# Softmax probabilities scaled tile by tile on GpSimd, a first pair loaded in groups, and later row sums

## The chip, the cores and the metric

The kernel runs on one core of one Trainium2 chip. The metric is the device time of one execution in microseconds (us); the median of three runs stands for the kernel. All times here are us unless marked ns. The engines are PE (TensorE's matmuls; PEld are its weight loads), DVE (VectorE), ACT (ScalarE), POOL (GpSimd) and SP (SyncE, which only issues DMAs here).

## What is computed

Three layers follow one another on 4 batches of 576 tokens. The first is an attention of 8 heads of 64: four heads with a local mask of 32 positions, four with a strided mask.

```python
scores = scale * np.matmul(q, k.transpose(0, 1, 3, 2))
scores = np.where(masks[None, :, :, :], scores, -1000000000.0)
scores = scores - np.max(scores, axis=-1, keepdims=True)
attn = np.exp(scores)
attn = attn / (np.sum(attn, axis=-1, keepdims=True) + 1e-09)
return np.matmul(attn, v).astype(np.float32)
...
theta = x @ w_theta
zr, zi = x * np.cos(theta), x * np.sin(theta)
y = np.einsum('ts,bsd->btd', w_tok_r, zr) + np.einsum('ts,bsd->btd', w_tok_i, zi)
u = x + y
x = u + np.maximum(u @ w_ch, 0.0)
```

The second layer, in the lower lines, mixes tokens with two 576x576 matrices and channels with one of 512x512. The third is a mixture of 4 causal attention experts, of which each token takes two.

## The kernel before

**Attention.** Only blocks that the masks leave are computed. Two heads go together as a pair (pairs 0 and 1 local, 2 and 3 strided), and a pair is cut into three groups of tiles: local tiles are 128 rows (64 queries of two heads) by 96 keys, three in a group; strided tiles are 108 rows by 54 keys, four, four and three in a group. `load_pair` loads q, k and the three v pieces of a pair with one DMA each. `attn_pair` does for every group: PE adds the mask (L185) and the scores `s` (L189) in PSUM; DVE takes the maximum `mx` (L203 or L210); ACT takes the exponential into `p`. Where `per_tile` holds (batch 0 but for pair 2, and the first group of each pair of batch 1), ACT does it tile by tile and adds up the rows itself (L206); else DVE subtracts (L211), ACT does all tiles in one instruction (L213), and DVE sums the rows (L214). DVE adds 1e-9 and takes the reciprocal `sm` (L215, L216). L217 multiplies all tiles of `p` at once by `sm`, spread over the columns: DVE does it in batch 0, GpSimd in batches 1 to 3. PE transposes the tiles of `p` into `tp` (L220), ACT or DVE copies them to `pt` (L224), PE multiplies with v into `av` (L243), and `av` is copied into X (L248, L250).

**Mixing.** Per batch and half h: `theta` (matmuls L265 to L267 on `th`, three for each product, since every factor is split into a high and a low part), sines on ACT, `rotate` (`xn` transposes L311, products `cs` on DVE, high and low parts `zhi`, `zlo`), and `tokens` (the matmuls on `y`, whose sums DVE adds to X at L350). `channels` follows one batch later, with the matmuls on `g`: eight groups of 12 matmuls, named g_b_m_n, in two PSUM buffers; DVE drains each with L372. The weights arrive as 64-bit numbers in pieces (`load64`) and are converted by ACT (L139, L102) and DVE (L140, L104, L106) during batch 0.

**Experts.** From about 350 us on; their code is not touched.

**Order.** Each engine runs its instructions in a fixed order. It is made when the program is built, by a scheduler that plays a timeline of all engines; `tc.issue_after` holds an instruction back until another is issued. So each edit can move instructions on every engine. The attention of batch b+1 is woven between the mixing of batch b. SP issues DMAs in its own fixed order, and one that waits for a buffer holds up those behind it.

Of the kernel before, what the change touches and what calls it, by code (L numbers as in the profile page):

```python
# [19 lines left out]
ALU = mybir.AluOpType  # L20
AX = mybir.AxisListType
PSUM = bass.MemoryType.PSUM

B, S, DM, HD, NE = 4, 576, 512, 64, 4
NT = 5
TW = [128, 128, 128, 128, 64]
HALF = S // 2
# [20 lines left out]
def fused_kernel(ctx: ExitStack, tc: tile.TileContext, ql, kl, vl, qs, ks, vs, wth, wtk, wch, wqk, wvg, wo, out):  # L48
    nc = tc.nc
# [95 lines left out]
    def per_tile(b, pair, g):  # L145

        return b == 0 and pair != 2 or b == 1 and g == 0
# [3 lines left out]
    def load_pair(b, pair, ain, qbufs, kbufs):  # L151
        local = pair < 2
        pj = pair % 2
        groups, rw, kw = (LOCAL, LQ, LK) if local else (STRIDED, RQ, RQ)
        nq = groups[-1][1]

        qt = ain.tile([128, 11 * 2 * RQ], F32, tag="q", bufs=qbufs, name=f"q_{b}_{pair}")
        qt = qt[:, :nq * 2 * rw].rearrange("p (n q) -> p n q", n=nq)
        kt = ain.tile([128, S + WPAD], F32, tag="k", bufs=kbufs, name=f"k_{b}_{pair}")
        kn = S + WPAD if local else S  # L160
        nc.sync.dma_start(qt, (ql if local else qs)[b, pj])
        nc.sync.dma_start(kt[:, :kn], (kl if local else ks)[b, pj])
        vgs = []
        for g, (j0, j1) in enumerate(groups):
            vg = ain.tile([128, 4, 2, HD], F32, tag="v", name=f"v_{b}_{pair}_{g}")
            nc.sync.dma_start(vg[:kw, :j1 - j0], (vl if local else vs)[b, pj, :, j0:j1])
            vgs.append(vg)
        loaded[b, pair] = qt, kt, vgs

    def attn_pair(b, pair, ps1, apl, deep):  # L170
        ps_of[b] = ps1
        local = pair < 2
        groups, rw, kw = (LOCAL, LQ, LK) if local else (STRIDED, RQ, RQ)
        qt, kt, loads = loaded[b, pair]
        xo = X[b][:, pair, :]
        done = []
        for g, (j0, j1) in enumerate(groups):
            vg = loads[g]
            n = j1 - j0

            wd = [min(rw, S - rw * j) for j in range(j0, j1)]
            mask = mask_l[:, min(g, 1):min(g, 1) + 3, :] if local else mask_s[:, 2 * (g // 2):2 * (g // 2) + n, :]
            rm = 2 * rw
            s = ps1.tile([128, 512], F32, tag="s", bufs=2 * deep, name=f"s_{b}_{pair}_{g}")
            nc.tensor.matmul(s[:rm, :n * kw], twice[pair // 2], mask, start=True, stop=False)  # L185
            for i in range(n):
                k0 = rw * (j0 + i)
                w = kw if local else wd[i]
                nc.tensor.matmul(s[:rm, i * kw:i * kw + w], qt[:, j0 + i, :], kt[:, k0:k0 + w], start=False, stop=i == n - 1)  # L189
            mx = apl.tile([128, 4], F32, tag="mx", name=f"mx_{b}_{pair}_{g}")  # L190
            sm = apl.tile([128, 4], F32, tag="sm", name=f"sm_{b}_{pair}_{g}")

            ss = s[:, 384:388] if per_tile(b, pair, g) else sm
            p = apl.tile([128, 3 * LK], F32, tag="p", name=f"p_{b}_{pair}_{g}")

            def tiles(v):
                return v[:rm, :n * kw].rearrange("p (n k) -> p n k", n=n)

            def each(v):
                return v[:rm, :n, None].to_broadcast([rm, n, kw])  # L200

            if per_tile(b, pair, g):
                peaks[b] = nc.vector.tensor_reduce(mx[:rm, :n], tiles(s), axis=AX.X, op=ALU.max, negate=True).ins  # L203
                nc.scalar.activation(mx[:rm, :n], mx[:rm, :n], AF.Copy, scale=SCALE)
                for i in range(n):
                    powers[b] = nc.scalar.activation(p[:rm, i * kw:(i + 1) * kw], s[:rm, i * kw:(i + 1) * kw], AF.Exp,  # L206
                                                     bias=mx[:rm, i:i + 1], scale=SCALE,
                                                     accum_out=ss[:rm, i:i + 1]).ins
            else:
                nc.vector.tensor_reduce(mx[:rm, :n], tiles(s), axis=AX.X, op=ALU.max)  # L210
                nc.vector.tensor_tensor(tiles(p), tiles(s), each(mx), op=ALU.subtract)  # L211
                with tc.issue_after(sins[b - 1, pair // 2]) if (b > 1 and pair % 2) else nullcontext():
                    nc.scalar.activation(p[:rm, :n * kw], p[:rm, :n * kw], AF.Exp, scale=SCALE)  # L213
                nc.vector.tensor_reduce(sm[:rm, :n], tiles(p), axis=AX.X, op=ALU.add)  # L214
            nc.vector.tensor_scalar_add(sm[:rm, :n], ss[:rm, :n], 1e-9)  # L215
            nc.vector.reciprocal(sm[:rm, :n], sm[:rm, :n])  # L216
            (nc.vector if b == 0 else nc.gpsimd).tensor_tensor(tiles(p), tiles(p), each(sm), op=ALU.mult)  # L217
            tp = ps1.tile([128, 512], F32, tag="t", bufs=deep, name=f"tp_{b}_{pair}_{g}")
            for i in range(n):
                turned = nc.tensor.transpose(tp[:kw, i * rm:(i + 1) * rm], p[:rm, i * kw:(i + 1) * kw],  # L220
                                             ident[:rm, :rm])
            pt = apl.tile([128, 8 * RQ], F32, tag="pt", name=f"pt_{b}_{pair}_{g}")
            copy = nc.vector.tensor_copy if b == 0 and g == 1 else nc.scalar.copy
            copy(pt[:kw, :n * rm], tp[:kw, :n * rm])  # L224
            done.append((j0, pt[:, :n * rm].rearrange("p (n h q) -> p n h q", n=n, h=2), wd, vg))
            if b == 0 or g == 2:

                for part in (done,) if b == 0 else (done[:2], done[2:]):
                    values(b, pair, part, xo, turned)
                done = []  # L230
# [33 lines left out]
    def mm3(ps, ahi, alo, bhi, blo, first, last):  # L264
        nc.tensor.matmul(ps, ahi, bhi, start=first, stop=False)  # L265
        nc.tensor.matmul(ps, ahi, blo, start=False, stop=False)  # L266
        return nc.tensor.matmul(ps, alo, bhi, start=False, stop=last)  # L267
# [66 lines left out]
            eng = nc.gpsimd if b > 0 else nc.vector  # L334
            halved[b, h] = eng.tensor_tensor(lo, zf, f(hi), op=ALU.subtract).ins  # L335

    us = {}

    def tokens(b, h):
        for n in range(2):  # L340
# [21 lines left out]
    def channels(b):  # L362
        for n in range(2):
            sl = slice(HALF * n, HALF * (n + 1))
            for m in range(4):
                g = ps1.tile([128, 512], F32, tag="acc", bufs=2, name=f"g_{b}_{m}_{n}")
                ms = slice(128 * m, 128 * m + 128)
                for c in range(4):
                    mm3(g[:, :HALF], wch_hi[:, c, ms], wch_lo[:, c, ms], us[c][0][:, sl], us[c][1][:, sl],
                        c == 0, c == 3)  # L370
                u = X[b][:, m, sl]
                nc.vector.scalar_tensor_tensor(u, g[:, :HALF], 0.0, u, op0=ALU.max, op1=ALU.add)  # L372

    halfpi = const.tile([128, 1], F32, name="halfpi")
    nc.gpsimd.memset(halfpi, math.pi / 2)
# [416 lines left out]
```

## Time and profile before

| | us |
|---|---|
| median of 3 runs (lowest, highest) | 556.71 (555.69, 557.0) |
| profiled execution | 555.94 |
| its span, first to last instruction | 553.8 |
| busy in the span: PE | 529.7 |
| busy: DVE, ACT, GpSimd | 400.9, 315.9, 188.5 |

The span is what the profile's views show; the profiled execution's time is 2.1 us longer. A line such as L217 is a line of the kernel before. Windows give each engine's busy time in a stretch and the clock that TensorE was granted in it (1.00 is 2.4 GHz, 0.50 is 1.2 GHz). The chain of waits follows the work that ended last back from the end. In a timeline, a bracket holds the engine's idle time before the instruction and what ended it.

### The profile page before, as it was taken

Reading aid. Unit: us, or ns where it says so; the run is one execution under the profiler, and the core shown is the slowest. Engines: PE = TensorE matmul, PEld = TensorE weight load, DVE = VectorE, ACT = ScalarE, POOL = GpSimd, SP = SyncE. Lnnn points to the kernel's source line nnn. Section 1 sums busy time; section 2 is a strip of 40 time slices with the busy share of each in tenths; the row PEclk is TensorE's granted clock in tenths of the full one; section 3 lists DMA queues with packets and bytes.
Section 4 is the critical chain, followed back from the end, with each engine's and each line's share of the span. In section 5 each row is a group of like instructions: output and inputs, shape, how many; then the busy total and the mean of one; then the engine's idle time right before and its main releaser. Section 6 shows DMA issues by size and latency. Waiting matters only on the chain.

```text
span 553.8 us, 12475 instructions
## 1 busy us (share of the span) xinstructions
PE 529.7 (96%) x4536; PEld 507.0 (92%) x4536; DVE 400.9 (72%) x1222; ACT 315.9 (57%) x904; POOL 188.5 (34%) x273
## 2 busy tenths in 40 slices
PE   6898999998999999999999999989999999999987
PEld 5778899998999999999999998879989999999987
DVE  4979997675775567675456443798988898888972
ACT  4977984426363163452246321576687767767873
POOL 1000013321562113551015533254456434625451
PEclk9959999999999999999999999999999999999999
DMA  9957243560202131001000011000001001100012
GB/s 286 320 180 262 81 161 107 168 197 1 90 23 68 32 132 33 24 24 43 17 0 1 28 33 40 1 1 2 1 10 59 22 1 44 44 2 11 33 45 86
DMA packets 20389, 37.53 MB, mean 68 GB/s; under 512 B 2904, under 2 KB 12296, under 8 KB 20328
## 3 DMA queue, kind: packets, MB, share of 16 engines
q1 hardware_dynamic: 20328, 36.73, 20.4%
q8 instruction: 36, 0.59, 0.5%
q14 instruction: 25, 0.20, 0.1%
HBM read 32.01 MB, written 4.72 MB: 66 GB/s over the span
## 4 chain that ended last, share of the span: by engine, by line
PE 74%; DVE 12%; ACT 8%; DMA 2%; issue 2%; POOL 1%; SPq 0%; DVEq 0%; POOLq 0%; ACTq 0%
PE y L265 7%; PE y L266 7%; PE y L267 7%; PE s L189 6%; PE av L243 4%; PE tp L220 3%; PE tp L624 3%; PE g L265 3%; PE g L267 3%; PE g L266 3%; PE th L265 3%; PE th L267 3%; PE th L266 2%; DVE nm L603 2%; PE o L580 2%; PE s L598 2%
## 5 line engine op out<-in xcount | busy, mean ns | idle before, releaser
L265 PE MATMUL y<-wtk_hi,zhi 128*128 128x288 f32 x288 | 85.8, 300 | 1.5 <-DVE cs L289 1.1
L266 PE MATMUL y<-wtk_lo,zhi 128*128 128x288 f32 x288 | 85.8, 298 | 0.0
L267 PE MATMUL y<-wtk_hi,zlo 128*128 128x288 f32 x288 | 85.3, 297 | 0.0
L217 POOL TENSOR_TENSOR p<-p,sm 128x288 f32<-128x288 f32 (+2 forms) x36 | 22.4, 628 | 150.3 <-PE y L267 73.2
L621 POOL TENSOR_SCALAR p<-p,sm,gt 128x256 f32<-128x256 f32 (+1 forms) x64 | 45.2, 709 | 52.5 <-DVE sm L619 32.5
L614 ACT ACTIVATE p<-s,nm 128x128 f32<-128x128 f32 (+2 forms) x96 | 49.6, 518 | 14.2 <-DVE nm L603 7.8
L265 PEld LDWEIGHTS y<-wtk_hi,zhi 128*128 128x128 f32 x288 | 54.0, 188 | 1.9 <-ACT wtk_hi L102 1.2
L266 PEld LDWEIGHTS y<-wtk_lo,zhi 128*128 128x128 f32 x288 | 54.2, 188 | 0.1
L335 POOL TENSOR_TENSOR zlo<-cs,zhi 128x512 fp32r<-128x512 f32 (+1 forms) x30 | 35.8, 1208 | 54.0 <-DVE zhi L331 43.2
L267 PEld LDWEIGHTS y<-wtk_hi,zlo 128*128 128x128 f32 x288 | 54.1, 188 | 0.1
L265 PE MATMUL th<-wth_hi,x_hi 128*128 128x256 f32 (+1 forms) x160 | 47.9, 300 | 0.6 <-ACT X L250 0.5
L603 DVE TENSOR_REDUCE nm<-s 128x1 f32<-128x128 f32 (+2 forms) x96 | 44.2, 468 | 5.5 <-PE s L601 4.4
L266 PE MATMUL th<-wth_lo,x_hi 128*128 128x256 f32 (+1 forms) x160 | 46.0, 288 | 0.0
L267 PE MATMUL th<-wth_hi,x_lo 128*128 128x256 f32 (+1 forms) x160 | 45.8, 290 | 0.0
L189 PE MATMUL s<-k,q 128*108 128x54 f32 (+2 forms) x320 | 42.8, 274 | 1.5 <-DMA k<-in_kl 1.5
L189 PEld LDWEIGHTS s<-k,q 128*108 128x108 f32 (+1 forms) x320 | 40.7, 196 | 2.5 <-issue 2.4
L224 ACT COPY pt<-tp 96x384 f32<-96x384 f32 (+2 forms) x44 | 21.0, 478 | 37.9 <-PE tp L220 37.6
L265 PE MATMUL pq<-x_hi,wqk_hi 128*128 128x288 f32 x128 | 39.8, 311 | 1.1 <-DVE q L549 1.0
L261 POOL TENSOR_TENSOR x_lo<-X,x_hi 128x576 fp32r<-128x576 f32 x20 | 29.8, 1495 | 32.2 <-DVE x_hi L259 25.8
L265 PE MATMUL g<-u_hi,wch_hi 128*128 128x288 f32 x128 | 38.9, 304 | 1.4 <-DVE X L372 1.4
L633 DVE TENSOR_TENSOR ptlo<-tp,pthi 128x128 fp32r<-128x128 f32 (+4 forms) x80 | 37.6, 478 | 1.2 <-ACT pthi L632 0.6
L266 PE MATMUL pq<-x_lo,wqk_hi 128*128 128x288 f32 x128 | 38.0, 297 | 0.0
(173 smaller groups left out, 1702.6 us busy)
## 6 DMA issues: line engine op xcount, KB each, us to landing
X<-in_wtk SPq DMA_DIRECT2D x18, 287.8 KB
q<-in_qs SPq DMA_DIRECT2D x8, 594.0 KB
q<-in_ql SPq DMA_DIRECT2D x8, 576.0 KB
v<-in_vl SPq DMA_DIRECT2D x24, 144.0 KB
out_t<-X SPq DMA_DIRECT2D x20, 128.0 KB
k<-in_kl SPq DMA_DIRECT2D x8, 304.0 KB
k<-in_ks SPq DMA_DIRECT2D x8, 288.0 KB
X<-in_wth SPq DMA_DIRECT2D x8, 255.8 KB
```

The lines of the kernel that those rows point to most:

```text
L189: nc.tensor.matmul(s[:rm, i * kw:i * kw + w], qt[:, j0 + i, :], kt[:, k0:k0 + w], start=False, stop=i == n - 1)
L217: (nc.vector if b == 0 else nc.gpsimd).tensor_tensor(tiles(p), tiles(p), each(sm), op=ALU.mult)
L243: nc.tensor.matmul(av[64 * h:64 * h + 64, c0:c0 + wi], vg[:w, i, h, :], pt[:w, i, h, :wi], start=True, stop=True)
L261: halved[name] = eng.tensor_tensor(lo, x, f(hi), op=ALU.subtract).ins
L265: nc.tensor.matmul(ps, ahi, bhi, start=first, stop=False)
L266: nc.tensor.matmul(ps, ahi, blo, start=False, stop=False)
L267: return nc.tensor.matmul(ps, alo, bhi, start=False, stop=last)
L335: halved[b, h] = eng.tensor_tensor(lo, zf, f(hi), op=ALU.subtract).ins
L603: nc.vector.tensor_reduce(nm[:w, t + ci:t + ci + 1], s[:w, :c1 - c0], axis=AX.X, op=ALU.max, negate=True)
L614: nc.scalar.activation(p[:w, c0:c1], scs[ci][:w, :c1 - c0], AF.Exp, bias=nm[:w, t:t + 1], scale=1.0, accum_out=acc)
L621: eng.tensor_scalar(p[:w, :kn], p[:w, :kn], sm[:w, t:t + 1], gt[:w, t, e:e + 1], op0=ALU.mult, op1=ALU.mult)
L633: nc.vector.tensor_tensor(dst(ptlo), src, f(dst(pthi)), op=ALU.subtract)
```

## The change

Three things change. The first pair of batch 0 is loaded by groups: q and k come in three DMAs each, a group of q and then the part of k that it needs. For pair 1 of batches 2 and 3, the row sums (L217 now) are held back until DVE's drain of the matmul group g of block 0 and second half (`gated[b - 2, 1, 0]`, now L377) is issued. The multiplication by the reciprocal is done by GpSimd in all batches, one instruction for each tile, with a column of `sm` as a scalar for each row (now L222) in place of one instruction for a group.

```diff
-        nc.sync.dma_start(qt, (ql if local else qs)[b, pj])
-        nc.sync.dma_start(kt[:, :kn], (kl if local else ks)[b, pj])
+        for j0, j1 in groups if (b, pair) == (0, 0) else [(0, nq)]:
+            nc.sync.dma_start(qt[:, j0:j1], (ql if local else qs)[b, pj, :, j0:j1])
+            k0, k1 = j0 * rw + (kn - S if j0 else 0), kn if j1 == nq else j1 * rw + kn - S
+            nc.sync.dma_start(kt[:, k0:k1], (kl if local else ks)[b, pj, :, k0:k1])
...
-                nc.vector.tensor_reduce(sm[:rm, :n], tiles(p), axis=AX.X, op=ALU.add)
+                with tc.issue_after(gated[b - 2, 1, 0]) if (b > 1 and pair == 1) else nullcontext():
+                    nc.vector.tensor_reduce(sm[:rm, :n], tiles(p), axis=AX.X, op=ALU.add)
             nc.vector.tensor_scalar_add(sm[:rm, :n], ss[:rm, :n], 1e-9)
             nc.vector.reciprocal(sm[:rm, :n], sm[:rm, :n])
-            (nc.vector if b == 0 else nc.gpsimd).tensor_tensor(tiles(p), tiles(p), each(sm), op=ALU.mult)
+            for i in range(n):
+                cols = p[:rm, i * kw:(i + 1) * kw]
+                nc.gpsimd.tensor_scalar(cols, cols, sm[:rm, i:i + 1], 1.0, op0=ALU.mult, op1=ALU.mult)
...
-                nc.vector.scalar_tensor_tensor(u, g[:, :HALF], 0.0, u, op0=ALU.max, op1=ALU.add)
+                gated[b, n, m] = nc.vector.scalar_tensor_tensor(u, g[:, :HALF], 0.0, u, op0=ALU.max, op1=ALU.add).ins
```

The order of the instructions moves on every engine in the first 350 us. On PE the experts' part keeps its order, but for one of the last output blocks. Three places follow; names end with a buffer's number, which differs between the programs, and the numbers ahead of it are batch, pair and group (p, sm, s, tp, pt), or batch, m and n (g).

DVE in batch 0, pair 2, around the third group's subtraction; first before, then now.

```order
L140 SCALAR_TENSOR_TENSOR X2_63<-X1_62,X2_63 128x256
L211 TENSOR_TENSOR p_0_2_2_438<-s_0_2_2_431,mx_0_2_2_436 108x162
L214 TENSOR_REDUCE sm_0_2_1_405<-p_0_2_1_406 108x4
L140 SCALAR_TENSOR_TENSOR X2_63<-X3_64,X2_63 128x256
L224 COPY pt_0_1_1_305<-tp_0_1_1_301 96x384
L217 TENSOR_TENSOR p_0_2_0_373<-p_0_2_0_373,sm_0_2_0_372 108x216
```

```order
L266 TENSOR_TENSOR x0_0_0_lo_634<-X0_61,x0_0_0_hi_633 128x576
L219 RECIPROCAL sm_0_2_0_388<-sm_0_2_0_388 108x4
L229 COPY pt_0_1_1_319<-tp_0_1_1_315 96x384
L213 TENSOR_TENSOR p_0_2_2_460<-s_0_2_2_453,mx_0_2_2_458 108x162
L218 TENSOR_SCALAR sm_0_2_1_424<-sm_0_2_1_424 108x4
L140 SCALAR_TENSOR_TENSOR X2_63<-X1_62,X2_63 128x256
```

The subtraction into p_0_2_2 stood three rows ahead of the copy of tp_0_1_1 and now stands behind it; the multiplication of p_0_2_0 is gone from DVE.

DVE in batch 1, up to the first reciprocal, sm_1_0_0, whose scaled tiles PE transposes first; first before, then now.

```order
L215 TENSOR_SCALAR sm_1_0_0_995<-s_1_0_0_989 128x3
L214 TENSOR_REDUCE sm_1_0_1_1017<-p_1_0_1_1018 128x3
L140 SCALAR_TENSOR_TENSOR X2_63<-X3_64,X2_63 128x256
L104 TENSOR_TENSOR wtk_lo_113<-X2_63,wtk_hi_112 128x288
L104 TENSOR_TENSOR wch_lo_115<-X2_63,wch_hi_114 128x256
L360 TENSOR_TENSOR u_0_0_lo_1288<-X0_61,u_0_0_hi_1287 128x288
L360 TENSOR_TENSOR u_0_1_lo_1292<-X0_61,u_0_1_hi_1291 128x288
L211 TENSOR_TENSOR p_1_0_2_1039<-s_1_0_2_1032,mx_1_0_2_1037 128x288
L216 RECIPROCAL sm_1_0_0_995<-sm_1_0_0_995 128x3
```

```order
L218 TENSOR_SCALAR sm_1_0_0_1027<-s_1_0_0_1021 128x3
L104 TENSOR_TENSOR wtk_lo_113<-X2_63,wtk_hi_112 128x288 x2
L340 TENSOR_TENSOR zlo_0_1_4_961<-cs_0_1_4_919,zhi_0_1_4_960 128x256
L140 SCALAR_TENSOR_TENSOR X2_63<-X3_64,X2_63 128x288
L217 TENSOR_REDUCE sm_1_0_1_1051<-p_1_0_1_1052 128x3
L212 TENSOR_REDUCE mx_1_0_2_1073<-s_1_0_2_1068 128x3
L140 SCALAR_TENSOR_TENSOR X2_63<-X3_64,X2_63 128x256
L219 RECIPROCAL sm_1_0_0_1027<-sm_1_0_0_1027 128x3
```

The reciprocal was row 180 of DVE's program and is now row 159: twelve of the 21 rows less are the multiplications of batch 0, and nine are conversions, subtractions and low parts that now come later.

DVE in batch 2, around the row sums of pair 1; first before, then now.

```order
L372 SCALAR_TENSOR_TENSOR X0_61<-g_0_2_0_1911,X0_61 128x288
L321 TENSOR_TENSOR cs_1_0_1_1723<-cs_1_0_1_1723,xn_1_0_1_2003 128x512
L214 TENSOR_REDUCE sm_2_1_0_2052<-p_2_1_0_2053 128x3
L214 TENSOR_REDUCE sm_2_1_1_2073<-p_2_1_1_2074 128x3
L215 TENSOR_SCALAR sm_2_1_0_2052<-sm_2_1_0_2052 128x3
L214 TENSOR_REDUCE sm_2_1_2_2094<-p_2_1_2_2095 128x3
L372 SCALAR_TENSOR_TENSOR X0_61<-g_0_3_0_1925,X0_61 128x288
L215 TENSOR_SCALAR sm_2_1_1_2073<-sm_2_1_1_2073 128x3
L216 RECIPROCAL sm_2_1_0_2052<-sm_2_1_0_2052 128x3
```

```order
L377 SCALAR_TENSOR_TENSOR X0_61<-g_0_2_0_1977,X0_61 128x288
L326 TENSOR_TENSOR cs_1_0_1_1783<-cs_1_0_1_1783,xn_1_0_1_2069 128x512
L377 SCALAR_TENSOR_TENSOR X0_61<-g_0_3_0_1991,X0_61 128x288
L377 SCALAR_TENSOR_TENSOR X0_61<-g_0_0_1_2005,X0_61 128x288
L217 TENSOR_REDUCE sm_2_1_0_2118<-p_2_1_0_2119 128x3
L217 TENSOR_REDUCE sm_2_1_1_2141<-p_2_1_1_2142 128x3
L217 TENSOR_REDUCE sm_2_1_2_2164<-p_2_1_2_2165 128x3
L326 TENSOR_TENSOR cs_1_0_2_1800<-cs_1_0_2_1800,xn_1_0_2_2077 128x512
L218 TENSOR_SCALAR sm_2_1_0_2118<-sm_2_1_0_2118 128x3
L218 TENSOR_SCALAR sm_2_1_1_2141<-sm_2_1_1_2141 128x3
L218 TENSOR_SCALAR sm_2_1_2_2164<-sm_2_1_2_2164 128x3
L377 SCALAR_TENSOR_TENSOR X0_61<-g_0_1_1_2019,X0_61 128x288
```

The three sums stood ahead of the fourth drain, of g_0_3_0. Now the fourth and the fifth, g_0_0_1, stand ahead of them, and the sixth, g_0_1_1, behind. PE's order has the transposes of this pair behind the last g, and had the first of them behind the sixth g.

## Rows read from the trace of the kernel before

**Rows 1.** Page, part 1: busy us (share of the span) xinstructions.
```profile
PE 529.7 (96%) x4536; PEld 507.0 (92%) x4536; DVE 400.9 (72%) x1222; ACT 315.9 (57%) x904; POOL 188.5 (34%) x273
```

**Rows 2.** Windows: stretch, its us, busy by engine, PEclk, DMA share, GB/s.
```profile
0.00:10.00 10.00, 5.24 (x22) 4.35 (x22) 3.49 (x13) 3.15 (x11) 2.57 (x15) 1.00 0.86 267
10.00:20.00 10.00, 9.99 (x100) 9.47 (x99) 7.99 (x30) 8.84 (x44) 0.00 (x0) 1.00 1.04 359
...
24.00:28.00 4.00, 1.89 (x35) 1.39 (x34) 4.00 (x16) 4.00 (x26) 0.00 (x0) 0.92 0.74 235
28.00:41.20 13.20, 12.14 (x108) 10.56 (x109) 10.43 (x31) 10.25 (x31) 0.00 (x0) 0.51 0.59 181
54.90:59.00 4.10, 2.83 (x22) 2.45 (x23) 4.07 (x12) 4.04 (x12) 0.00 (x0) 1.00 0.12 26
```

**Rows 3.** Chain that ended last, to 59 us: start us, us, what.
```profile
1.16 4.61 DMA k<-in_kl
...
38.50 5.23 DMA X<-in_wtk
...
58.90 0.37 PE y L265
```

**Rows 4.** Waits of PE, whole span: engine line <- releaser: us, times, longest.
```profile
PE s L185 <- DVE mask_l L80: 3.3, 1, 3.3
...
PE s L189 <- DMA k<-in_kl: 1.5, 1, 1.5
PE g L265 <- DVE X L372: 1.4, 1, 1.4
...
PE tp L220 <- POOL p L217: 0.7, 1, 0.7
```

**Rows 5.** Timeline of batch 2, ACT, DVE, PE: start us, us, instruction [idle <-releaser].
```profile
132.82 1.11 ACT L213 ACTIVATE p<-p 128x288 f32<-128x288 f32 x3
...
133.30 0.81 DVE L214 TENSOR_REDUCE sm<-p 128x3 f32<-128x288 f32 x2 [2.26 <-ACT p L213]
...
134.96 0.40 PE L265 MATMUL g<-u_hi,wch_hi 128*128 128x288 f32 x1 [1.39 <-DVE X L372]
```

**Rows 6.** Groups by form: operation, shapes xcount | busy us, mean ns | idle before.
```profile
L621 POOL TENSOR_SCALAR p<-p,sm,gt 128x256 f32<-128x256 f32 x16 | 9.4, 585 | 18.5 <-DVE sm L619 14.4 <-DVE sm L618 1.5 <-ACT q L548 1.0
L621 POOL TENSOR_SCALAR p<-p,sm,gt 128x512 f32<-128x512 f32 x16 | 12.3, 771 | 5.1 <-DVE sm L619 3.7 <-PE pq L267 1.0 <-ACT tmp L585 0.2
L654 POOL TENSOR_SCALAR ohi<-X 128x256 fp32r<-128x256 f32 x9 | 3.6, 404 | 10.2 <-DVE X L586 8.3 <-issue 1.5 <-POOL k L554 0.4
L654 POOL TENSOR_SCALAR ohi<-X 128x320 fp32r<-128x320 f32 x7 | 3.4, 486 | 3.1 <-DVE X L586 3.1
L217 POOL TENSOR_TENSOR p<-p,sm 128x288 f32<-128x288 f32 x18 | 12.8, 716 | 128.6 <-PE y L267 73.2 <-DVE sm L216 37.4 <-DVE sm L215 11.3
L214 DVE TENSOR_REDUCE sm<-p 128x3 f32<-128x288 f32 x16 | 6.9, 440 | 4.4 <-ACT p L213 4.2
```

**Rows 7.** Timeline: first L217 of batch 1, its transpose, first GpSimd tensor_scalar.
```profile
76.28 1.40 POOL L217 TENSOR_TENSOR p<-p,sm 128x288 f32<-128x288 f32 x1 [73.16 <-PE y L267]
...
77.74 0.53 PE L220 MATMUL tp<-ident,p 128*96 128x128 f32 x3 [0.70 <-POOL p L217]
...
354.38 0.42 POOL L554 TENSOR_SCALAR k<-k 64x288 fp32r<-64x288 f32 x1 [1.13 <-ACT k L552]
```

**Rows 8.** Line L217: duration ns min/median/max, first and last start, forms.
```profile
L217 DVE TENSOR_TENSOR p<-p,sm x12: 286/411/461, 9.9 to 31.5; 128x288 f32<-128x288 f32 x6, 108x216 f32<-108x216 f32 x4, 108x162 f32<-108x162 f32 x2
```

**Rows 9.** Timeline, end of the attention of batch 0: ACT, DVE, PE, DVE.
```profile
28.80 0.22 ACT L206 ACTIVATION_READ_ACCUMULATOR p<-s,mx 108x1 f32 x1
...
31.17 0.61 DVE L217 TENSOR_TENSOR p<-p,sm 108x216 f32<-108x216 f32 x2
...
32.73 1.46 PE L220 MATMUL tp<-ident,p 108*54 108x108 f32 x7
...
36.58 0.46 DVE L259 CAST x_hi<-X 128x576 fp32r<-128x576 f32 x1 [2.29 <-ACT X L250]
```

More of the change, by code (lines that the diff above doesn't have):

```diff
@@ L335, in rotate @@
             halved[b, h] = eng.tensor_tensor(lo, zf, f(hi), op=ALU.subtract).ins
-    us = {}
+    us, gated = {}, {}
     def tokens(b, h):
```

## Prediction

> **What bounds the kernel now.** I read the page first: PE is busy 529.7 us, 96% of the span of 553.8, so the time is PE's work plus some 24 us in which PE has nothing to run [rows 1]. The profiled execution took 555.94 us, 2.1 us more than its span; the median of the runs shown is 556.71 us, 0.77 us above it. I make the sum against 555.94 and carry the difference over to the median.
>
> The windows show where PE's idle time is [rows 2]. In the first 10 us PE is busy 5.24; from 24 to 28 us only 1.89 of 4; from 54.9 to 59 us 2.83 of 4.1. From 59 us on PE is almost never idle until 350 us, and what is left lies in the experts' part. The first matmul on y at 58.90 us is the point to watch: whatever brings it forward ends the kernel as much earlier, and after it only a wait of PE counts. In the chain of waits the steps up to it are: the load of k (4.61 us), scores, attention, and a load of wtk that is issued at 38.50 us and takes 5.23 us [rows 3]. The loads before it wait until the attention of batch 0 has left its buffers, and its last copy releases DVE's x_hi at 36.58 [rows 9], so the attention's end carries the 58.90.
>
> The list of PE's waits gives the terms [rows 4]: 1.5 us for the first k, behind 3.3 for a mask, 1.4 us where a matmul on g waits for DVE's L372, 0.7 us where a transpose waits for GpSimd's L217. The change touches all three.
>
> **The late row sums.** In batch 2, DVE's three row sums L214 wait for ACT's exponentials; DVE sits idle 2.26 us until 133.30 and three L372 stand behind them. g uses two PSUM buffers, so PE stands idle for 1.39 us until 134.96 [rows 5]. In the new order the fourth and the fifth L372 stand ahead of the sums, and only the sixth is behind. The fourth g would then be drained as PE finishes it, and the sixth group of 12 matmuls could start at 133.6. It would end at 135.2; the sums end at about 135.0 (three of 0.44 from the exponentials' end at 133.9, 132.82 + 1.11, less what overlaps), then some 1.1 for L321 and the additions, so the sixth drain ends by 136.6, when the eighth g needs it (136.8). I take the whole wait: **-1.4 us**. Bounds: -1.4, and 0 if the same wait comes back at the eighth g. In batch 3 the list shows no such wait, so the edit is worth nothing there. The transposes of this pair move behind the last g by some 4 us of PE work, which also covers the longer scaling.
>
> **The price of one scaled tile.** The trace has no GpSimd tensor_scalar of 128x96 or 108x54 with one scalar from memory. Below: L654, with constants alone, 0.404 us at 256 columns and 0.486 at 320, that is 1.28 ns a column; drawn down to 96 and 54 columns it is 0.20 and 0.15 us. Above: L621, with two scalars from memory, 0.585 at 256 and 0.771 at 512, 0.73 ns a column, 0.47 and 0.44 us [rows 6]. One scalar lies halfway: **0.33 and 0.29 us**. A local group (three tiles) is then 1.0 us against 0.716 for the one instruction now, a strided one of four tiles 1.17, of three 0.88; on DVE in batch 0 the one instruction takes 0.41 at the median [rows 8]. The outermost value is 0.585 a tile, if an instruction costs what its shortest row with scalars shows. A batch has 40 tiles, so four batches are 160 instructions and about 49 us on an engine that is now busy 188.5 of 553.8 us, L217's present work in it [rows 1]; it is no bound.
> The Trainium skill (GPSIMD Engine Reference, Performance pitfalls for Q7 kernels) speaks against such splitting: every small read command costs about 102 cycles that don't overlap the one before. By that figure one scalar adds an estimated 0.085 us to the lower rows, a tile 0.28 or 0.23 us, and the sum below would be about 0.3 us lower; no row here has one scalar alone, and 0.181 us lie between L621 and L654 at 256 columns for two.
>
> **Batches 1 to 3.** PE's new order leaves 4 us or more of PE work between a group's scores and its transposes. The chain between them is four instructions over all columns of about 0.44 each, such as the sum L214 [rows 6], two small ones, and the scaling of 1.0 to 1.2: some 3.3, which fits. The one wait seen is the first L217 of batch 1, which took 1.40 us, double the rest, and let PE stand 0.70 us at 77.74 [rows 7]. The first GpSimd tensor_scalar at 354.38 took its usual 0.42, so the new first instruction should not be slow, and DVE reaches the reciprocal with some nine instructions fewer ahead of it (its twelve multiplications of batch 0 apart). PE comes to this transpose about 1 us earlier, DVE about 4 us (nine of 0.45). **-0.7 us**; bounds -0.7 and +0.7 (the wait doubles, if DVE's nine are waited for later).
>
> **Batch 0.** Three parts. (a) The first pair by groups: k lands 4.61 us after its issue, and the scores start at about 5.9 [rows 3]; a third of q and k, behind a mask that is ready after 3.3, lets PE start at about 3.9, a head start of 2.0 us. SP issues four more DMAs before the rest. But DMA is busy 0.86 of the first 10 us and all of the next [rows 2], and the bytes of pairs 1 to 3 come no earlier. ACT, which is busy 8.84 of the 10 us from 10 to 20 and all of 24 to 28 [rows 2], meets the gaps: I walk its new order with the durations of the rows and find it idle 0.6 us at the second group, 0.6 at the first group of pair 1 (whose k lands as before), and 1.0 in pair 2, where DVE's subtraction for the third group now stands behind the copy of a transpose. That is 2.2 of 2.0: nothing is left. (b) DVE loses twelve multiplications of 0.41 us, 4.9 us [rows 8]. It is full from 24 to 28 us, but so is ACT [rows 2], and DVE then stands idle 2.29 us before the last x_hi [rows 9]; the saving is hidden by ACT. (c) The last two groups: their exponentials end at 29.02, DVE's two multiplications at 31.78, PE's seven transposes take 1.46 at the lower clock [rows 9]. Seven tiles on GpSimd are 2.0 instead of 0.61 us, but each transpose can start behind its own tile, so about 1.2 of the 1.4 us more is covered: **+0.2 us**. For the attention's end together: +0.2, bounds -2.0 (the head start is kept whole) and +2.3 (seven tiles of 0.585 are 4.1, less 0.61 and 1.2).
>
> The experts' part keeps its code; on PE only one of the last output blocks changes place: 0.
>
> **Sum.** -1.4 - 0.7 + 0.2 = -1.9. The profiled execution would take 554.0, the median **554.8 us**, 0.34% less. About 0.3% (1.7 us) is what a measurement of this kernel can tell from no change, so the forecast lies close to that line.
>
> **Rivals.**
> 1. The head start survives: ACT is the one engine that holds batch 0, and the gaps that I found are filled by other work. For it: ACT's share. Against it: the DMA share. -1.4 - 0.7 - 2.0 = -4.1, 552.6 us.
> 2. A tile costs 0.585: the tail of batch 0 grows by 2.3, and -1.4 - 0.7 + 2.3 = +0.2, 556.9 us; if the wait of batch 1 stays as well, 557.6. For it: L621 is the only row with scalars from memory. Against it: L554, 288 columns with constants, takes 0.42.
> 3. The wait of batch 2 comes back at the eighth g, because the sixth drain stands behind the sums and my margin there is only 0.2 us: -0.7 + 0.2 = -0.5, 556.2 us.
> 4. Slower: TensorE's clock. From 24 to 28 us PE was busy 1.89 of 4, and then the granted clock was half until 41.2, over 13.2 us [rows 2]. There it costs little, since DMA and ACT hold the path. From 54.9 to 59 us PE was busy 2.83 of 4.1 and the clock stayed whole. If that second gap becomes as empty as the first, the half clock falls on y, where PE has no slack, and 13.2 us do the work of 6.6: +6.6 - 1.9 = +4.7, 561.4 us. Against it: nothing in the new order makes the gap before y clearly longer.
>
> **How the numbers follow.** Forecast 0.50, with a range of its own of 553.6 to 556.0; rivals 0.10, 0.18, 0.15 and 0.07. Faster: 0.38 of the forecast, the first rival, almost nothing else: 0.48. Same: the rest of the forecast, most of the third rival and half the second: 0.35. Slower: the fourth rival, the upper half of the second and a little more: 0.17. The range goes from the first rival, 552.6, to the second with its wait, 557.4; above lie the fourth rival and the end of the second, below a little of the first.
>
> **What would show it.** First scores near 3.9 us. GpSimd's tiles at 0.33 and 0.29 us; near 0.58 is rival 2. The last copy of batch 0's attention near 36.7 and the first y near 59.1; at 34.6 and 57 it is rival 1. No wait of PE on g; one of over 1 us at the eighth is rival 3. No wait at the first transpose of batch 1. A clock of 1.00 from 59 us to 350; 0.5 there is rival 4. A new PE wait of over 1 us between 60 and 350 us at any other place would make the prediction wrong by its length.

## The result and the profile after

The changed kernel takes **562.0 us** (median of 4 runs, 560.93 to 563.24) against 556.65 (before, now 4 runs too): a ratio of 1.0103, interval 1.0072 to 1.0133. It is slower by 1%, above the range of the prediction. Medians below are over all executions, while a ratio leaves out those over 1.5% above the fastest of the same kernel, so the two can differ. Its profiled execution took 562.49 us with a span of 560.7, 6.9 more than the span before.

The page of the changed kernel, part 1, against [rows 1]:

```profile
PE 532.7 (95%) x4536; PEld 507.3 (90%) x4536; DVE 393.7 (70%) x1210; ACT 315.5 (56%) x904; POOL 224.8 (40%) x397
```

PE is busy 3.0 us longer; the other 3.9 us are new idle time. The windows of the changed kernel (stretch, its us, busy of PE, PEld, DVE, ACT, POOL, granted clock, DMA share, GB/s), against [rows 2]:

```profile
0.00:10.00 10.00, 6.34 (x26) 5.13 (x26) 3.96 (x15) 4.38 (x17) 3.59 (x19) 1.00 0.73 216
10.00:20.00 10.00, 6.25 (x52) 5.79 (x52) 2.41 (x8) 4.90 (x27) 2.18 (x7) 1.00 1.01 281
...
28.00:41.20 13.20, 8.77 (x90) 5.20 (x86) 8.27 (x26) 9.43 (x44) 9.30 (x18) 0.62 0.53 175
41.20:50.00 8.80, 8.29 (x65) 8.15 (x66) 6.56 (x17) 6.31 (x17) 0.00 (x0) 0.60 0.69 211
60.00:80.00 20.00, 17.17 (x132) 16.11 (x131) 19.87 (x50) 18.63 (x53) 0.00 (x0) 1.00 0.27 78
```

From 0 to 10 us PE does more than before (6.34 for 5.24): the head start is there, with the first scores at 3.55 us. From 10 to 20 it is busy 6.25, where it was 9.99, and DVE and ACT starve with it (2.41 and 4.90 for 7.99 and 8.84). DMA is as full as before there (1.01 for 1.04) and yet moves 281 GB/s for 359. From 28 to 41.2 us PE is busy 8.77 for 12.14, and GpSimd, idle before, works 9.30 of 13.2.

The waits of PE in the changed kernel name both places (engine, line, releaser: us, times, longest):

```profile
PE s L191 <- DMA k<-in_kl: 3.9, 2, 3.6
PE tp L225 <- POOL p L222: 3.5, 7, 0.9
PE s L187 <- DVE mask_l L80: 3.3, 1, 3.3
PE pv L272 <- DVE x_lo L266: 2.1, 2, 1.1
PE s L187 <- DVE p L213: 1.4, 2, 1.1
```

The first, second and fifth are new or larger. The chain of the changed kernel shows where they are on the path:

```profile
5.40 7.99 DMA k<-in_kl
13.52 2.85 PE s L191 x12
...
30.60 1.73 POOL p L222 x2
...
34.44 2.14 POOL p L222 x4
```

The k on the path is no longer that of the first pair [rows 3], but that of pair 1: issued at 5.40, landed at 13.39. Before, PE went on from the first pair's scores to pair 1's at 10.04 without a gap, as the chain of the kernel before shows:

```profile
5.91 4.13 PE s L189 x18
10.04 0.01 issue
10.04 1.57 PE s L189 x6
```

Four starts follow the loss through the profiled executions: DVE's last x_hi of batch 0, PE's first matmul on y, the first on g and the last product L265 (now L270) on g. For the changed kernel the last three come from the lists of the tiles y and g (durations in ns, first and last start in us):

```profile
L270 PE MATMUL y<-wtk_hi,zhi x288: 289/295/407, 64.6 to 332.7; 128*128 128x288 f32 x144
...
L270 PE MATMUL g<-u_hi,wch_hi x128: 288/295/398, 132.9 to 345.4; 128*128 128x288 f32 x128
```

| kernel | last x_hi | first y | first g | last g |
|---|---|---|---|---|
| before | 36.6 | 58.9 | 125.0 | 338.6 |
| changed | 43.4 | 64.6 | 132.9 | 345.4 |
| difference | +6.8 | +5.7 | +7.9 | +6.8 |

So 5.7 us are lost up to the first y, 2.2 more up to the first g, 1.1 come back by the last g, and the rest of the span is as long as before (+6.9 at the end). How far single executions can be trusted here: one program that was profiled three times (experiments 7 to 9) had its first y at 59.6, 60.3 and 61.0, so a difference of 1 us at that point says little; from the first y to the first g its three executions agree within 0.1.

### The profile page after: what moved, and what is told of

Same layout as the page of the kernel before. It is cut to its first block, busy times and chain, and to the rows that moved or that the text cites. A ratio compares the mean times of both kernels' runs of the same rounds, so it can differ in the third digit from the quotient of the medians.

```text
span 560.7 us, 12614 instructions
## 1 busy us (share of the span) xinstructions
PE 532.7 (95%) x4536; PEld 507.3 (90%) x4536; DVE 393.7 (70%) x1210; ACT 315.5 (56%) x904; POOL 224.8 (40%) x397
## 4 chain that ended last, share of the span: by engine, by line
PE 69%; DVE 15%; ACT 7%; DMA 3%; issue 2%; POOL 2%; SPq 1%; DVEq 0%; POOLq 0%; ACTq 0%
PE y L270 6%; PE y L271 6%; PE y L272 6%; PE s L191 4%; PE av L248 4%; PE g L272 3%; PE g L270 3%; PE tp L629 3%; PE g L271 3%; PE th L270 3%; PE th L272 3%; PE tp L225 3%; PE th L271 2%; DVE nm L608 2%; PE o L585 2%
## 5 line engine op out<-in xcount | busy, mean ns | idle before, releaser
L222 POOL TENSOR_SCALAR p<-p,sm 108x54 f32<-108x54 f32 (+1 forms) x160 | 59.6, 390 | 134.4 <-DVE sm L219 64.5
L270 PE MATMUL y<-wtk_hi,zhi 128*128 128x288 f32 x288 | 86.7, 302 | 0.9 <-DVE cs L294 0.5
L270 PEld LDWEIGHTS y<-wtk_hi,zhi 128*128 128x128 f32 x288 | 54.1, 188 | 1.7 <-DVE cs L294 0.8
L270 PE MATMUL th<-wth_hi,x_hi 128*128 128x256 f32 (+1 forms) x160 | 48.2, 302 | 0.6 <-ACT X L255 0.5
L270 PE MATMUL pq<-x_hi,wqk_hi 128*128 128x288 f32 x128 | 39.8, 311 | 1.0 <-DVE q L554 0.8
L270 PE MATMUL g<-u_hi,wch_hi 128*128 128x288 f32 x128 | 38.9, 304 | 0.0
```

Source lines behind the costliest of these rows:

```text
L222: nc.gpsimd.tensor_scalar(cols, cols, sm[:rm, i:i + 1], 1.0, op0=ALU.mult, op1=ALU.mult)
```

## The experiments

The theories: **A**, GpSimd's tiles stand still in batch 0 while DVE runs instructions with both inputs in SBUF; **B**, the groups' load delays the transfers behind it. The first four kernels take the parts of the change back.

**1. The scaling of batch 0 back on DVE.**

```diff
-            for i in range(n):
-                cols = p[:rm, i * kw:(i + 1) * kw]
-                nc.gpsimd.tensor_scalar(cols, cols, sm[:rm, i:i + 1], 1.0, op0=ALU.mult, op1=ALU.mult)
+            if b:
+                for i in range(n):
...
+            else:
+                nc.vector.tensor_tensor(tiles(p), tiles(p), each(sm), op=ALU.mult)
```

> The changed kernel with the scaling of batch 0 back on DVE, one instruction for a group; groups' load, late sums and GpSimd's tiles in batches 1 to 3 stay. Theory A (in batch 0 GpSimd's tiles stand still while DVE runs an instruction with both inputs in SBUF, such as L140, L106 and x_lo; PE then waits 3.5 us in all for L222 and its clock falls to half until about 48 us): the waits of PE for L222 go, the last x_hi of batch 0 comes at 38 to 39.5 instead of 43.4, the time is 556.5 to 558.5. Theory B (the small transfers of the first pair delay the k of pair 1 by 3.6 us, and all of the loss is that delay and the clock behind it): the last x_hi stays at 41 or later, the time at 560 to 562.

559.16 us, ratio 1.0063 (1.0033 to 1.0092). The waits for L222 in batch 0 are gone, but PE still waits 4.9 us for the k of pair 1, which takes 8.26 us to land. The last x_hi comes at 41.4, the first y at 63.1. Of the two expectations theory B's is nearer on the place and A's on the time: both parts cost. The wait can cost more than its own length. In this execution PE stood idle 4.95 us until 13.81, and in the window around it the granted clock was at half (1.2 GHz) for some 7 us, which the changed kernel's window, at 1.00, doesn't show:

```profile
10.00:20.00 10.00, 6.10 (x50) 5.55 (x50) 3.07 (x11) 3.86 (x22) 0.00 (x0) 0.66 0.98 306
```

**2. The first pair loaded whole.** The changed kernel with the two lines of the load as before.

> The changed kernel with the first pair loaded whole again (one transfer of q, one of k); late sums and GpSimd's tiles in all batches stay. Theory A (tiles locked out in batch 0): PE still waits 3 us or more for L222, first y at 62 or later, 559 to 562. Theory B (small transfers): k of pair 1 lands by 10 us as before, the wait of 3.6 us at the second pair goes, first y near 60 or earlier, 555 to 557.5.

556.67 us, ratio 1.0015 (0.9994 to 1.0035). The window from 10 to 20 us is back:

```profile
10.00:20.00 10.00, 9.90 (x79) 9.26 (x79) 5.64 (x23) 8.10 (x39) 5.59 (x18) 1.00 1.04 355
```

First y at 59.6, 0.7 later than before, though PE waits for GpSimd's tiles five times, 1.8 us in all. Theory B, then, for the larger part.

**3. Both taken back.** Late row sums, and GpSimd's tiles in batches 1 to 3 only.

> The changed kernel with both taken back: batch 0 scales on DVE and the first pair is loaded whole; what is left is late sums and GpSimd's tiles in batches 1 to 3. Theory A and B alike: first y at 58.5 to 59.5, no wait of PE on g in batch 2: 554.5 to 555.7. Rival C (the tiles of batches 1 to 3 cost as well, since new waits of about 2 us stand between the first y and the first g of the changed kernel): 556.5 to 558.

554.0 us, ratio 0.9951 (0.9933 to 0.997), below the expectation's lower end. First y at 59.4, no wait of PE on g. The transpose that waited 0.70 us [rows 7] waits 0.28. Rival C falls.

**4. The late row sums alone.**

> The kernel before with the late row sums alone (scaling as before: DVE in batch 0, one GpSimd instruction for a group after it). By the prediction's first term the 1.39 us wait on g goes and nothing takes its place: 555.0 to 555.6. Rival: the wait comes back at a later g or at a transpose: 556.2 to 557.

552.74 us, ratio 0.9947 (0.9921 to 0.9974): faster than both kernels and than expected, and as fast as the third within the intervals, so the tiles of batches 1 to 3 are worth nothing that shows. No wait on g is left. The orders of the two kernels are the same up to batch 2, and in the profiled executions the stretch from the first to the last g is 211.9 us for 213.6. The gain of 3.9 in the medians is more than the wait. About 1 us of the rest may be the clock of the experts' part: in the profiled executions of this kernel and of the kernel before it is 0.91 from 366 to 386 us, in experiment 3's 1.00, and from the last g to the end of the span the former two take 215.1 and 215.2 us, the latter 214.1. The profiled execution (554.39, mean clock 0.984) is slower than the median, and the five fastest have 0.986 or 0.987. Where the remainder lies stays open.

**5. The groups' load alone.** The kernel before with only the load changed.

> The kernel before with the groups' load of the first pair alone (scaling and row sums as before). If the load is the larger cost of the change (the pair of runs with and without it differed by 1.1%): PE's wait for the k of pair 1 is 3 us or more and the time 560 to 563. If its cost hangs on the late sums' order: 556 to 558.

564.89 us at the median, above the expectation, ratio 1.0103 (1.0058 to 1.0148): by the ratio as slow as the whole change. PE waits 4.0 us for the k, and the first y is at 64.0. Theory B holds without the other parts.

The ten times run from 557.73 to 569.66, and the mean granted clocks go with them. In experiments 1, 5 and 10, which all have the groups' load, 13 of 31 executions have a mean clock of 0.972 or less, and these are all the times of 562 and more; in the four kernels with a whole load (2, 3, 4 and 6) it is 1 of 39. The four runs of the changed kernel lie between, at 0.975 to 0.981. So part of the load's price in the timed runs goes with the clock. The profiles of 1 and 10 show one place: the clock falls while PE waits for the k of pair 1.

The starts of these kernels' profiled executions, put side by side:

| kernel | last x_hi | first y | first g | last g |
|---|---|---|---|---|
| 1: groups' load, DVE in batch 0 | 41.4 | 63.1 | 129.3 | 341.8 |
| 2: whole load, tiles in batch 0 | 37.5 | 59.6 | 127.7 | 340.1 |
| 3: neither | 37.8 | 59.4 | 125.8 | 338.3 |
| 4: late sums alone | 37.7 | 59.5 | 125.6 | 337.5 |
| 5: groups' load alone | 42.1 | 64.0 | 130.6 | 344.2 |

The groups' load puts the first y back by 3.7 (1 against 3), 5.0 (changed against 2) or 5.1 (5 against before). The tiles of batch 0 put it back by 0.2 (2 against 3) or, with the groups' load, 1.5 (changed against 1). The differences of 0.2 and 1.5 are not clear of what one program varies by. From the first y to the first g it is 66.1 to 66.6 us in these kernels without tiles in batch 0, and 68.1 and 68.3 with them: 2 us. The tiles are not needed for that, though: experiments 6 to 10, which scale batch 0 on DVE, take 68.4 to 68.7.

**6. Four more transfers without small pieces.** Is it the number of transfers or their size? Late row sums and a whole load, and behind k:

```diff
+        if (b, pair) == (0, 0):
+            spare = ain.tile([1, 128], F32, tag="spare", bufs=1, name="spare")
+            for i in range(4):
+                nc.sync.dma_start(spare[:, 32 * i:32 * i + 32], ql[0, 0, i:i + 1, 0, :32])
```

> Late row sums, the first pair loaded whole, and four transfers of 128 bytes more on SP between the first pair's k and its v (they move nothing that is used): the number of transfers of the groups' load without its small pieces. Theory H (four more issues, and four more places taken among the transfers that may be under way, are the cost): SP issues the k of pair 1 at about 5.4 us, it lands after 11 us, PE waits 2 us or more for it, and the time is 555 to 558. Theory S (the pieces of 1536, 896 and 768 bytes for each partition move slower than whole rows of 4608 and 2432): the k of pair 1 lands by 10.5 us, PE waits under 1 us more than before, 552.5 to 554.5.

555.68 us, ratio 0.9985 (0.9955 to 1.0015). SP issues the k of pair 1 at 5.94, later than in the changed kernel, and yet pair 1's scores start at 10.89, the window from 10 to 20 us shows PE at 9.81 with 359 GB/s, and the first y stands at 59.2. So four more issues alone don't make the delay; what is left is the pieces. The summary of the DMAs in the first 6 us, of the changed kernel and then of this one:

```profile
DMA packets 940, 1.01 MB, mean 169 GB/s; under 512 B 102, under 2 KB 940, under 8 KB 940
```
```profile
DMA packets 589, 1.30 MB, mean 216 GB/s; under 512 B 76, under 2 KB 333, under 8 KB 589
```

The kernel before moved 1.35 MB there. The time is above theory S's range, and within theory H's, whose other signs (a landing after 11 us, a wait of 2 us) are absent. It is lost elsewhere: PE waits 1.44 us for DVE's p, at the place where the changed kernel does, since DVE's order in batch 1 came out otherwise.

```profile
70.85 0.30 PE L189 MATMUL s<-mask_l,twice 128*128 128x288 bf16 x1 [1.44 <-DVE p L215]
```

**7. Only the first group apart.** Two more transfers in place of four: `for j0, j1 in [groups[0], (groups[0][1], nq)]`.

> Late row sums, and of the first pair only the first group of q and k loaded apart, the other two groups together: two transfers more in place of four, and half of the small pieces. First scores at 3.6 us as in the changed kernel. Theory H and theory S alike put the k of pair 1 about half as late (1.5 to 2 us in place of 3.6): 554 to 557. Rival: the earlier start of PE is worth more than that delay and the time falls below the late sums alone, under 552.5.

563.78 us, ratio 1.0104 (1.0059 to 1.015), but the seven times fall in two heaps, 556.7 to 558.0 and 563.8 to 564.9. The upper heap is not the half clock: its mean granted clocks are 0.996 to 0.999, those of the lower 0.983 to 0.987. The profiled execution is of the lower one: first y at 60.3, k of pair 1 landed 6.55 us after its issue. The rival falls: even there the head start wins nothing.

**8 and 9. The same kernel again, for the upper heap.**

> The kernel with the first group loaded apart once more, for one profile: its seven times fell at 557 to 558 and at 564 to 565, the latter with a granted clock of almost 1. If this one falls at 564: theory M (the transfers move fewer GB/s at a full DMA share in that execution) shows fewer than 300 GB/s from 10 to 20 us and a wait of 3 us or more for a k; theory O (another order of landings, or a stretch behind batch 0) shows 350 GB/s there and the loss elsewhere. At 557: nothing is told.

556.02 us, in the lower heap, so nothing is told of the upper. Its window from 10 to 20 us moves 309 GB/s at a DMA share of 1.05.

> The kernel with the first group loaded apart, a third look, since the second fell at 556. If the profiled execution falls near 564: theory M shows fewer than 300 GB/s at a full DMA share from 10 to 20 us and a wait of 3 us or more for a k; theory O shows 350 GB/s there and the loss elsewhere. Near 557 nothing is told and it stays open.

557.66 us over 8 runs, ratio 1.0051 (0.999 to 1.0112), with the same two heaps (the upper again at a clock of 0.998); the profiled execution is again of the lower one, so it stays open what the upper one is. One thing did come out. The window from 10 to 20 us of this execution, and of the one in 7:

```profile
10.00:20.00 10.00, 7.46 (x82) 6.13 (x82) 5.55 (x20) 6.67 (x38) 0.00 (x0) 1.00 1.05 296
```
```profile
10.00:20.00 10.00, 9.06 (x70) 8.48 (x70) 4.94 (x17) 6.16 (x33) 0.00 (x0) 1.00 1.05 353
```

With experiment 8, one program moved 296, 309 and 353 GB/s in three executions, at the same DMA share.

**10. The pieces of k issued by ACT.** `nc.scalar.dma_start` for the three pieces of k.

> Late row sums and the first pair by groups, with the three pieces of k issued by ACT in place of SP: the same six pieces, but SP issues one transfer more than before, not four. Theory H in its first half (SP's issue time): the k of pair 1 is issued at 4 us and lands by 10.5, PE's wait for it is under 1.5 us, 552 to 554. Theory S (or the places taken): it lands at 12 us or later, PE waits 2.5 us or more, 556 to 560.

557.88 us, ratio 1.0018 (0.9998 to 1.0038), between the two expectations. The profiled execution (564.7) is far above that median, so its k, landed 8.23 us after the issue at 4.66, and its PE wait of 3.8 us need not hold for the others. After that wait the clock stays at half up to 52 us. Against the kernel with SP's issues (1) the ratio is lower by 0.4%, of which the clock may be a part (2 of 10 executions here have 0.972 or less, 5 of 11 there); the first pair loaded whole (3, 4) stays well ahead. The test doesn't decide. Its windows say one thing more:

```profile
0.00:10.00 10.00, 5.60 (x26) 4.57 (x26) 4.42 (x16) 4.52 (x17) 2.57 (x15) 1.00 0.81 242
10.00:20.00 10.00, 6.98 (x43) 6.32 (x44) 3.35 (x11) 4.15 (x24) 0.00 (x0) 0.57 0.99 277
```

In the first 10 us it moved 242 GB/s, as much as experiment 6 (244), where pair 1's scores began at 10.89 and not at 13.02. So the late k is not explained by fewer bytes moved up to then alone.

**11. The price of a tile.** The whole computation is left out; eight GpSimd tiles run beside eight DVE instructions of each kind.

```diff
+            if i < pool:
+                nc.gpsimd.tensor_scalar(t, t, c[:, 0:1], 1.0, op0=ALU.mult, op1=ALU.mult)
+            if dve:
+                dve()
```

> A kernel that leaves the whole computation out and only measures: eight of GpSimd's tile instructions (128x96, a column of scalars) alone, then beside eight DVE instructions of 288 columns: with both inputs in SBUF, with one of the two in PSUM, a copy SBUF to SBUF, a row maximum of SBUF; then DVE's two-input instructions alone, and GpSimd alone again. Theory A (GpSimd is locked out while DVE runs an instruction with two inputs in SBUF): the tile is 0.345 us alone, beside PSUM and beside the row maximum; 0.6 us or more beside two SBUF inputs. Rival (the long tiles of batch 0 have another cause, such as their own reads or the DMAs): 0.31 to 0.36 in all phases.

The list of the tile's line, a window for each phase: alone, beside two SBUF inputs, beside one input in PSUM (durations in ns, shortest, median, longest):

```profile
L87 POOL TENSOR_SCALAR t<-t,c x8: 347/347/347, 2.7 to 5.8; 128x96 f32<-128x96 f32 x8
...
L87 POOL TENSOR_SCALAR t<-t,c x8: 421/424/450, 7.0 to 10.6; 128x96 f32<-128x96 f32 x8
...
L87 POOL TENSOR_SCALAR t<-t,c x8: 347/347/348, 11.8 to 14.9; 128x96 f32<-128x96 f32 x8
```

Beside copies and row maxima it was 347 too. Of these kinds only two SBUF inputs disturb the tile, as theory A says, but by 0.08 us and not by 0.26. Each of DVE's instructions here needs the result of the one before; that the gaps between them let each tile in is likely, and experiment 12 takes the gaps away.

**12. The price without such gaps.** DVE multiplies two SBUF inputs into four tiles in turn, over 288 and then 576 columns.

> As the first price kernel (the whole computation is left out), but with nothing in a row depending on the one before: eight GpSimd tiles on four buffers, alone, beside twelve DVE multiplications of two SBUF inputs over 288 columns, beside eight over 576 columns, and alone again. The first price kernel's tiles took 0.42 to 0.45 us beside two SBUF inputs, and GpSimd and DVE took turns. Theory A (each tile stands still until the DVE instruction under way has ended): a tile takes 0.31 to 0.35 alone, about as long as one DVE instruction more when DVE leaves no gap: 0.6 to 0.7 beside 288 columns, 0.9 to 1.1 beside 576. Rival (a slowdown by a fixed share): 0.42 to 0.45 in both.

The tile's line beside 288 columns, beside 576, and alone:

```profile
L75 POOL TENSOR_SCALAR t<-t,c x7: 536/822/823, 5.3 to 10.0; 128x96 f32<-128x96 f32 x7
...
L75 POOL TENSOR_SCALAR t<-t,c x5: 345/1422/1427, 11.5 to 16.0; 128x96 f32<-128x96 f32 x5
...
L75 POOL TENSOR_SCALAR t<-t,c x11: 344/345/345, 19.0 to 22.8; 128x96 f32<-128x96 f32 x11
```

The rival of a fixed share falls: a tile of 0.345 us takes 0.82 and 1.42, that is 0.48 and 1.08 more, and DVE's instructions take 0.484 and 0.758 each at the median. The tile's time grows with the length of DVE's instruction, and by more than one of them at 576 columns. In both phases GpSimd gets one tile done for every two of DVE's.

## Why the prediction was wrong, step by step

**The step that failed** is part (a) of batch 0. It let the head start of 2.0 us be eaten up by gaps, "nothing is left", with bounds from -2.0 to nothing worse, and it took it that pair 1's k "lands as before". The head start came (first scores at 3.55), but the k landed at 13.39, some 3.4 us after PE had needed it before. Counted over three pairs of profiled executions, the load puts the first y back by 3.7 to 5.1 us; in the timed runs it costs 1.1% (1.0063 against 0.9951) and 0.9% (1.0103 against 1.0015), 6.2 and 4.9 us of 556, and 1.0% by itself (experiment 5). In some executions a half clock behind PE's wait is in that price. I had noted that the DMA was busy 0.86 of the first 10 us [rows 2] and that SP issues four more, and drew only the upside's loss from it. The pieces of a group are 192 KB of q and 96 of k (112 for the first), SP issues one every 0.47 us, and in the first 6 us 1.01 MB moved in place of 1.35. That the load delays this k is shown, with the number of issues as the sole cause ruled out by experiment 6. How the pieces do it is not: in the one profile of experiment 10 as many bytes had moved by 10 us as in experiment 6, and the k was still late. That the full DMA then moves 277 to 306 GB/s from 10 to 20 us, where kernels with a whole load move 352 to 359, is seen in every profile with three pieces (the changed kernel, 1, 5, 10), but 296, 309 and 353 also in three executions of one kernel; its cause stays open.

**The price of one scaled tile** was right as far as it went: 0.33 and 0.29 were estimated, and undisturbed tiles take 0.345 and 0.31. What failed is that one price was taken for all. In batch 0's tail the median is 0.571 and the longest 1.147 (the list of L222 from 30 to 42 us of the changed kernel):

```profile
L222 POOL TENSOR_SCALAR p<-p,sm x14: 310/571/1147, 30.6 to 40.1; 108x54 f32<-108x54 f32 x14
```

The timeline of the changed kernel, of GpSimd and DVE around two of them, shows why:

```profile
31.12 0.76 DVE L266 TENSOR_TENSOR x_lo<-X,x_hi 128x576 fp32r<-128x576 f32 x1
...
31.17 1.15 POOL L222 TENSOR_SCALAR p<-p,sm 108x54 f32<-108x54 f32 x1
...
31.80 0.42 DVE L106 SCALAR_TENSOR_TENSOR wth_lo<-X,wth_hi 128x256 fp32r<-128x256 f32 x1
...
32.30 0.31 POOL L222 TENSOR_SCALAR p<-p,sm 108x54 f32<-108x54 f32 x1
```

The first tile begins just after DVE's x_lo and lasts until x_lo and the conversion behind it are over; the next, with DVE idle, takes 0.31. The longest tile of all stands in experiment 2: it takes 2.07 us beside two such conversions (L106) and an x_lo, with short DVE instructions between them and no gap.

```profile
24.67 2.07 POOL L220 TENSOR_SCALAR p<-p,sm 108x54 f32<-108x54 f32 x1
```

Two SBUF inputs are not the only form that disturbs: beside DVE's cast x_hi, which has one, a tile of the changed kernel took 0.58.

```profile
35.96 0.58 POOL L222 TENSOR_SCALAR p<-p,sm 108x54 f32<-108x54 f32 x1
35.97 0.47 DVE L264 CAST x_hi<-X 128x576 fp32r<-128x576 f32 x1
```

The Trainium skill has a rule on this (SBUF — State Buffer, SBUF: two separate sides): GpSimd and DVE share a port pair; the one that starts first, be it a DVE instruction with two SBUF inputs, takes it for its whole length, and the other "fully blocks". Experiments 11 and 12 agree: 0.347 us beside a PSUM input, 0.82 and 1.42 beside two SBUF inputs. In the latter a tile waited for two of DVE's instructions, not for one, and in experiment 2 for more. I weighed a rule on the cost of small instructions and not this one, which spoke against the change in batch 0, where DVE converts weights.

The sign of it stood in my own rows. The first L217 of batch 1 took 1.40 us, "double the rest" [rows 7], and I took it for a slow first instruction. The timeline of DVE in the kernel before, at that time:

```profile
76.41 0.41 DVE L104 TENSOR_TENSOR wch_lo<-X,wch_hi 128x256 fp32r<-128x256 f32 x1
76.74 0.41 DVE L140 SCALAR_TENSOR_TENSOR X<-X,X 128x256 uint32<-128x256 uint32 x1
77.08 0.45 DVE L203 TENSOR_REDUCE mx<-s 128x3 f32<-128x288 f32 x1
```

**Part (c), +0.2 for the tail**, is not contradicted with a whole load (first y +0.2, 2 against 3), and was 1.3 us too low behind the groups' load (1.5, changed against 1), where tiles met DVE's conversions as shown above; neither is clear of what one program varies by. As the tiles took nearly twice the price that the sum used, the agreement with a whole load is luck. In the timed runs the tiles of batch 0 cost 0.64% (2 against 3) and 0.40% (changed against 1), the next point with them.

**Not foreseen at all:** DVE's order in batch 1 came out otherwise, and 2 us are lost between the first y and the first g. The timeline of PE in the changed kernel shows the three waits:

```profile
69.88 0.40 PE L270 MATMUL y<-wtk_hi,zhi 128*128 128x288 f32 x1 [0.52 <-DVE cs L294]
...
76.49 0.30 PE L187 MATMUL s<-mask_l,twice 128*128 128x288 bf16 x1 [1.06 <-DVE p L213]
...
85.32 0.51 PE L225 MATMUL tp<-ident,p 128*96 128x128 f32 x3 [0.49 <-ACT mx L206]
```

The prediction had named "a new PE wait of over 1 us between 60 and 350 us" as what would make it wrong; the second is one. I followed the order around three places and not the scores of batch 1 on PE. With and without the tiles of batch 0 the loss comes and goes (2 against 3, changed against 1), but experiments 6 to 10 have it without them. So it belongs to an order that several edits bring about and not to GpSimd's tiles as such; which edit tips it stays open.

**The late row sums (-1.4)** did what was said: no wait on g is left in the changed kernel or in 1 to 4, and from the first to the last g it is 211.9 to 212.5 us for 213.6, a gain of 1.1 to 1.7. Rival 3 falls. **Batch 1 (-0.7):** the wait of 0.70 is 0.28 in experiment 3, a gain of 0.4.

**The other rivals.** The first, that the head start survives, falls. The second had the tile's price for the tail nearly right (0.585 against 0.571), for another reason, and not the place of most of the loss. The fourth, the half clock on y, did not occur in the profiled execution: the clock is 1.00 from 50 us to 350, and the half clock from 28 to 50 (0.62 and 0.60 in the windows) lies on the emptier stretch and on the matmuls on theta.

Summed from the profiled executions: 5.0 for the load (changed against 2), 0.7 up to y for the rest (2 against before), 2.2 behind it, less 1.1 on g, make the 6.8 at the last g. The first two are differences of single executions and good to about 1 us.

## What to carry to other kernels

Cutting a load to start earlier can put back the transfers behind it, as it did here: price the first wait behind the pieces, not only the head start, and let the bound go to the bad side. Before giving an elementwise step to GpSimd, look at what DVE runs at that time: beside its instructions with two SBUF inputs a tile took from 1.2 to over 6 times as long here (0.42 for 0.347, 2.07 for 0.31), the most where DVE left no gap. One GpSimd row that is double the rest is worth a look at DVE's timeline. When several edits go in together, build each alone: the best time here is that of the row sums alone, 0.5% faster than before. And before a loss after a reordered program is put down to one edit, look whether other orders have it too.

## What the runs showed that was not expected

- At a DMA share of about 1.0 from 10 to 20 us the bytes moved differ by a quarter, 277 to 359 GB/s; in three executions of one program they were 296, 309 and 353. A full share doesn't say how fast the transfers are.
- In two profiles (experiments 1 and 10) the clock fell to half while PE waited 4.9 and 3.8 us for a load early in the kernel; in two others (the changed kernel, 5), with waits of 3.6 and 4.0, it did not.
- GpSimd and DVE took turns in a fixed pattern when neither left a gap: one tile for two DVE instructions, 0.82 us beside 288 columns and 1.42 beside 576. With DVE instructions that follow from one another the tile lost only 0.08 us; in the kernel one took 2.07 us in place of 0.31.
